# A feed-forward whose first group takes the weights in two halves, and cumulative sums by triangle matmuls

## The chip, the core and the metric

One core of one Trainium2 chip runs one program. Its engines work in parallel, each through its own list of instructions in order: PE (TensorE) multiplies matrices, ACT (ScalarE) evaluates functions, DVE (VectorE) does elementwise work, POOL (GpSimd) only fills constants here, and SP (SyncE) issues all the transfers (DMA). Semaphores tie the lists together. The metric is the time of one execution on the device, in microseconds (us); lower is better.

## The reference

A linear attention with a complex decay is followed by a feed-forward. With 4 batches, 8 heads, 768 time steps and head size 48:

```python
for t in range(S):                      # S = 768
    ar, ai = a_re_n[:, :, t, :, None], a_im_n[:, :, t, :, None]     # capped at magnitude 0.999
    S_re, S_im = ar*S_re - ai*S_im + kv_t, ar*S_im + ai*S_re        # kv_t = outer(k_t, v_t)
    y[:, :, t] = einsum('bhd,bhde->bhe', q[:, :, t], S_re)
x = y.transpose(0, 2, 1, 3).reshape(B * S, H * D)                   # 3072 tokens of 384
h = x @ w_in                                                        # 384 -> 2048, weights in float64
g = maximum(h, 0) + log1p(exp(-abs(h)))                             # softplus
out = g @ w_out                                                     # 2048 -> 384
```

## The kernel before, in words

Time is cut into six *groups* of 128 steps. A group holds 4 *chunks*, one for each batch, of 128 tokens; its 512 tokens go through the feed-forward together. The kernel has two kinds of work.

*Attention.* `pre` turns the decays of a *slice* into running products: the logarithm of the magnitude and the angle of each step (ACT and DVE, 128 features on the partitions), then their cumulative sums over the 128 steps by `TENSOR_TENSOR_SCAN` on DVE (L484), then exp, sine and cosine (ACT), by which q and k are multiplied (L507, L530, L532). The first group has four slices of one batch (tiles 128x384), the others two slices of two batches (128x768). `chunk` then moves q and k to a layout by head with ten small transfers on SP's queue (L567), forms the scores on PE (`sc`, L613), masks them on DVE (L616), forms the outputs (`y`, L644 from the state and L647 from the scores), and casts y to the feed-forward's input `xt` as a rounded part and a rest (L655 or L656, L657). For the next group PE transposes k (`tr`, L590) and adds k's products with v to the state (`kv`, L668).

*Feed-forward.* `moe` takes a group through 16 *steps* of 128 hidden features. A step is nine 128x512 matmuls into a tile `h` (three feature blocks by three products of rounded parts and rests, L703), the softplus (ACT L708 to L710, DVE L711), a split of its result into `gh` and `gl` (L713 on DVE or L714 on ACT, L715 on DVE), and two steps later nine matmuls into the accumulators o0, o1, o2 (L727). There are two tiles `h`, so the third step's first matmul waits until L711 of the first has read its tile. At the end of a group `fin` copies o0 to o2 (DVE L741 and ACT L739) into buffers of the tag "lt", of which there are two, and sends them to the output (L742).

*Weights.* They come as 8-byte numbers in 16 blocks (eight `wi`, eight `wo`, two steps each, 768 KB of raw words). A block takes three DVE instructions on bits (L352, L355, L358), a rounding cast (L365 on ACT, or L367 on DVE) and a subtraction on DVE (L369). `inspect` reads all weights once more (`seen`) for a check on their size; `verdict` adds the checks up at the end with one small matmul (`pn`, L821), and only if one of them had failed a slow general path would run.

*The order.* All this is recorded as tasks with keys from the table `K`. `Planner.order` plays them through with estimated durations, on each engine the ready task of the lowest key first, and the program is written in that order; the engines keep to it whatever the real times are. Where PE has nothing ready between two marks (`gate`, and the first matmul into an accumulator, `opener`) the planner writes in a *filler*, a 128x128 matmul that nobody reads (L753, from L777 of the changed kernel); an f32 matmul of this kind appears as two records in a trace.

Of the kernel before, what the change touches and what calls it, by code (L numbers as in the profile page):

```python
# [21 lines left out]
P = 128  # L22
# [19 lines left out]
NAHEAD = 4  # L42
# [234 lines left out]
class Prog:  # L277
# [15 lines left out]
    def consts(self):  # L293
# [22 lines left out]
        self.toks = dram.tile([B, S, DM], F32, tag="toks", name="toks")  # L316
        self.chk = c.tile([P, self.nchk], F32, tag="chk", name="chk")

    def weights(self):
# [4 lines left out]
        for j in range(2 * NWP):  # L324
# [74 lines left out]
    def pre(self, si):  # L399
# [97 lines left out]
        def acc(j):  # L497
            part = b0 % 2 if m == 1 else None
            a = (car[j], part) if m == 1 else car[j]
            return dict(r=[] if first else [car[j]], w=[] if last else [a])  # L500
# [178 lines left out]
    def moe(self, xt, dst, key, dkey):  # L679
# [404 lines left out]
```

## Time and profile before

| | |
|---|---|
| time, median of 3 runs (lowest to highest) | 626.48 us (623.68 to 626.62) |
| the profiled execution's own time | 620.65 us |
| its span, first to last instruction | 618.9 us |
| PE busy | 577.4 us, 93% |
| DVE busy, ACT busy | 459.7 us (74%), 417.6 us (67%) |
| mean granted PE clock | 0.994 of 2.4 GHz |

The shares are means over stages that differ: PE is filled up from 20 us on, at first largely by fillers, and DVE is nearly full until some 180 us and half empty in the last 100. A row of the stage view gives the busy time of each engine in a stretch of time, so it tells which engine the stretch belongs to.

### The profile page before, as it was taken

To read this page: it belongs to the slowest core of one execution; us is meant where nothing else is said; L and a number is where in the kernel's file an instruction comes from. 1 tells how busy PE (TensorE), PEld (TensorE's weight loads), DVE (VectorE), ACT (ScalarE), POOL (GpSimd) and SP (SyncE) were. 2 spreads that over 40 slices of the span, in tenths; PEclk is the share of its full clock that TensorE was granted. 3 is DMA by queue.
4 is the path that set the end of the run, shared out by engine and by line. 5 is a ranking of instruction groups with operands and counts; after the bars stand their busy time and mean duration, and the time that the engine had idled before them with its cause. 6 is when DMAs were issued, how large, how long until landed. Compare 5 with 4: busy or idle time off the path is not lost.

```text
span 618.9 us, 11061 instructions
## 1 busy us (share of the span) xinstructions
PE 577.4 (93%) x4298; PEld 483.6 (78%) x4298; DVE 459.7 (74%) x702; ACT 417.6 (67%) x769; POOL 1.8 (0%) x16
## 2 busy tenths in 40 slices
PE   0699897999989999999999999999999999999994
PEld 0698886887877888878888888887887788888883
DVE  6898899998987988896778867888784535454442
ACT  8954658668549777785775954869884989345441
POOL 1000000000000000000000000000000000000000
PEclk9999998999999999999999999999999999999998
DMA  8778722252342524341343314251357873010002
GB/s 324 316 166 293 216 88 56 62 169 65 105 138 63 141 85 121 107 103 52 118 117 120 87 30 140 70 181 56 92 154 231 245 235 121 2 51 1 0 2 56
DMA packets 50076, 73.95 MB, mean 119 GB/s; under 512 B 5728, under 2 KB 42080, under 8 KB 50016
## 3 DMA queue, kind: packets, MB, share of 16 engines
q1 hardware_dynamic: 50016, 73.16, 39.0%
q8 instruction: 36, 0.59, 0.4%
q14 instruction: 24, 0.20, 0.1%
HBM read 49.55 MB, written 4.72 MB: 88 GB/s over the span
## 4 chain that ended last, share of the span: by engine, by line
PE 55%; ACT 14%; DVE 12%; DMA 9%; SPq 5%; issue 3%; DVEq 0%; ACTq 0%
PE h L703 21%; PE o L727 20%; SPq L567 4%; DMA x<-dense_dram 4%; PE sc L613 4%; PE o L753 3%; DMA raw_wo<-w_out_dram 3%; ACT L802 3%; PE kv L668 2%; PE y L647 2%; PE y L644 2%; DVE lt L711 2%; ACT lt L710 1%; ACT lt L709 1%; ACT lt L708 1%
## 5 line engine op out<-in xcount | busy, mean ns | idle before, releaser
L703 PE MATMUL h<-xt,wi 128*128 128x512 f32 x864 | 220.6, 401 | 6.7 <-DVE lt L711 6.1
L727 PE MATMUL o<-gh,wo 128*128 128x512 f32 x576 | 197.6, 400 | 0.0
L703 PEld LDWEIGHTS h<-xt,wi 128*128 128x128 f32 x864 | 160.5, 190 | 46.0 <-DVE lt L711 9.1
L711 DVE SCALAR_TENSOR_TENSOR lt<-h,lt 128x512 f32<-128x512 f32 x96 | 66.0, 689 | 96.3 <-ACT lt L710 96.0
L727 PEld LDWEIGHTS o<-gh,wo 128*128 128x128 f32 x576 | 108.5, 188 | 25.5 <-issue 1.2
L708 ACT ACTIVATE lt<-h 128x512 f32<-128x512 f32 x96 | 56.7, 591 | 95.5 <-PE h L703 82.8
L727 PE MATMUL o<-gl,wo 128*128 128x512 f32 x288 | 113.7, 395 | 0.2 <-DVE gl L715 0.2
L710 ACT ACTIVATE lt<-lt,one 128x512 f32<-128x512 f32 x96 | 69.2, 722 | 1.8
L715 DVE TENSOR_TENSOR gl<-lt,gh 128x512 fp32r<-128x512 f32 x96 | 66.2, 689 | 2.0
L727 PEld LDWEIGHTS o<-gl,wo 128*128 128x128 f32 x288 | 54.3, 189 | 11.9 <-DVE gl L715 0.5
L709 ACT ACTIVATE lt<-lt 128x512 f32<-128x512 f32 x96 | 60.6, 633 | 1.8
L613 PE MATMUL sc<-qk 96*128 96x128 f32 x384 | 48.4, 277 | 2.9 <-DMA qk<-x 1.6
L613 PEld LDWEIGHTS sc<-qk 96*128 96x128 f32 x384 | 46.1, 192 | 5.1 <-issue 2.2
L484 DVE TENSOR_TENSOR_SCAN t<-hold,t 128x384 f32<-128x384 bf16 x48 | 43.8, 946 | 2.6 <-ACT t L512 1.9
L713 DVE TENSOR_SCALAR gh<-lt 128x512 fp32r<-128x512 f32 x90 | 38.2, 425 | 9.4 <-PE o L727 3.9
L753 PE MATMUL o<-ident 128*128 128x128 f32 x334 | 41.5, 282 | 0.0
L753 PEld LDWEIGHTS o<-ident 128*128 128x128 f32 x334 | 40.1, 198 | 0.7 <-issue 0.6
L802 ACT ACT_TABLE_LOAD x28 | 35.9, 1283 | 0.4
L616 DVE TENSOR_TENSOR a<-sc,mask 128x512 f32<-128x512 f32 x48 | 31.9, 685 | 4.7 <-PE sc L613 4.5
L668 PEld LDWEIGHTS kv<-v,kt 128*96 128x96 f32 x320 | 29.9, 165 | 3.5 <-ACT s L674 1.4
L668 PE MATMUL kv<-v,kt 128*96 128x64 f32 (+1 forms) x320 | 29.8, 246 | 1.3 <-DMA v<-vpad_dram 1.3
L530 DVE TENSOR_TENSOR x<-x,t 128x1536 f32<-128x1536 f32 (+1 forms) x14 | 21.3, 1526 | 9.5 <-ACT t L517 9.5
(84 smaller groups left out, 585.8 us busy)
## 6 DMA issues: line engine op xcount, KB each, us to landing
x<-dense_dram SPq DMA_DIRECT2D x20, 768.0 KB, 5.4
qk<-x SPq DMA_DIRECT2D x96, 144.0 KB, 3.3
raw_wi<-w_in_dram SPq DMA_DIRECT2D x8, 768.0 KB, 9.6
raw_wo<-w_out_dram SPq DMA_DIRECT2D x8, 768.0 KB, 11.1
seen<-w_in_dram SPq DMA_DIRECT2D x16, 384.0 KB, 3.9
seen<-w_out_dram SPq DMA_DIRECT2D x16, 384.0 KB, 4.3
v<-vpad_dram SPq DMA_DIRECT2D x24, 224.0 KB, 2.8
out_dram<-o SPq DMA_DIRECT2D x18, 256.0 KB, 2.9
```

Of the source, the lines that this page charges most:

```text
L484: V.tensor_tensor_scan(out()[:, s], self.hold, inc()[:, s], 0.0, ALU.mult, ALU.add)
L613: PE.matmul(psc()[:, hh * P : (hh + 1) * P], q[:, h, CH:], q[:, h, :CH], start=True, stop=True)
L668: PE.matmul(kv()[: 2 * D, s], k[:, h, :, :].rearrange("p c d -> p (c d)"), v[:, s], start=h == 0, stop=h == H - 1)
L703: PE.matmul(h()[:, :n], w()[:, q, i, fs], x()[:, i, :n], start=k == 0, stop=k == 3 * NI - 1)
L708: add("ACT", a1(n) - 0.04, lambda: A.activation(tv(), h(), AF.Abs), k, r=[h], w=[t])
L709: add("ACT", a1(n), lambda: A.activation(tv(), tv(), AF.Exp, scale=-1.0), k, w=[t], tab="log")
L710: add("ACT", a1(n, 1), lambda: A.activation(tv(), tv(), AF.Ln, bias=self.one), k, w=[t], tab="log")
L711: add("DVE", d1(n), lambda: V.scalar_tensor_tensor(tv(), h(), 0.0, tv(), ALU.max, ALU.add), k, r=[h], w=[t])
L715: add("DVE", d1(n), lambda: V.tensor_tensor(gl(), tv(), gh().bitcast(F32), ALU.subtract), k, r=[t, gh], w=[gl])
L727: PE.matmul(acc[m]()[:, :n], w()[:, wq, f % 2, ms], x(), start=f == 0 and q == 0, stop=f == NF - 1 and q == 2)
L753: self.nc.tensor.matmul(self.acc0[0]()[:, :P], self.ident, x, start=True, stop=True)
L802: nc.scalar.preload_act_table_set(TABLES[table])
```

## The change

1. The feed-forward runs in seven *segments* instead of six (`SEGS`): the first group with the first eight steps, the second group whole, the first group with its last eight steps, then the other groups. At the end of the first segment its three partial sums go out to a scratch in device memory (`park`); at the end of the third they are read back and added on DVE (L757). 
2. In the first group, the cumulative sums are matmuls with an upper triangle of ones (`sums`, L497 of the changed kernel): the decays of this group now come from the host with time on the partitions, and a product with the triangle sums over time and turns the tile round in one go. The sums stand in PSUM, in tiles borrowed from `h`, o1 and o2, and ACT and DVE read them there. The eight scans of the group go.
3. The gate for fillers is the first triangle matmul instead of a filler behind L507 of the first slice.
4. `fin` takes its copies from the tag "t" (five buffers) instead of "lt" (two), and each copy may go to ACT or DVE.
5. A raw weight block lies in its own block's place instead of another block's or `xt`'s.
6. The table `K` is new throughout, and the planner's constant for a matmul is 0.02 instead of 0.0134 us above its columns.

```diff
-NAHEAD = 4
+SEGS = [(0, 0, NF // 2), (1, 0, NF), (0, NF // 2, NF)] + [(g, 0, NF) for g in range(2, NGRP)]
...
+        self.park = dram.tile([DM, GT], F32, tag="park", name="park")
...
-            shape = [P, n * self.wwords]
-            if j < 2 * NWP - NAHEAD:
-                raw = Buf(self.wpool, f"w{kind}{b + NAHEAD // 2}", shape, I32, f"raw_{tag}")
-            else:
-                raw = Buf(self.p, f"xt{j % 2}", shape, I32, f"raw_{tag}", 2)
+            raw = Buf(self.wpool, tag, [P, n * self.wwords], I32, f"raw_{tag}")
...
-            if not first:
-                V.tensor_tensor(i3[:, :, 0], i3[:, :, 0], car[j](), ALU.add)
+            V.tensor_tensor(i3[:, :, 0], i3[:, :, 0], car[j](), ALU.add)
...
-        st = m * sc(W // m) + (0.1 if first else 0.25)
-
...
-        a = acc(0)
-        add("DVE", st, lambda: scan(0, v1, v1), at(), r=a["r"], w=a["w"] + [t1])
-        add("ACT", a1(W), lambda: A.activation(cc()[:, :, 0, :], n3(v1()), AF.Exp), at(), r=[t1], w=ca, tab="log")
-        add("ACT", a1(W), lambda: A.activation(cc()[:, :, 1, :], n3(v1()), AF.Exp, scale=-1.0),
-            at(), r=[t1], w=ca, tab="log")
...
+        def sums(j, tag, bufs, src, key):
+            ps = Buf(self.ps, tag, [P, 512], F32, f"sum{j}_{si}", bufs)
+            v = lambda: ps()[:, :W]
+
+            def mm():
+                for i in range(NI):
+                    c = slice(i * P, (i + 1) * P)
+                    PE.matmul(ps()[:, c], src[1]()[:, c], self.mask, start=True, stop=True)
+
+            t = add("PE", 0.69, mm, key, r=[src[0]], w=[ps])
+            return ps, v, t
+
+        def keep(j, ps, v, key):
+            c = car[j]
+            add("DVE", 0.1, lambda: V.tensor_copy(
+                c().rearrange("p (i b) -> p i b", b=2)[:, :, b0 % 2], n3(v())[:, :, CH - 1]), key, r=[ps], w=[(c, b0 % 2)])
+
+        if first:
+            lb, vl, opener = sums(0, "h", 2, (t1, v1), at())
+            if si == 0:
+                self.gate = opener
+        else:
+            lb, vl = t1, v1
+            add("DVE", st, lambda: scan(0, v1, v1), at(), r=[car[0]], w=[t1] + ([] if last else [car[0]]))
+        add("ACT", a1(W), lambda: A.activation(cc()[:, :, 0, :], n3(vl()), AF.Exp), at(), r=[lb], w=ca, tab="log")
+        add("ACT", a1(W), lambda: A.activation(cc()[:, :, 1, :], n3(vl()), AF.Exp, scale=-1.0),
+            at(), r=[lb], w=ca, tab="log")
+        if first:
+            keep(0, lb, vl, at())
         add("DVE", d1(2 * W), lambda: V.tensor_tensor(ss(), ss(), cc(), ALU.mult), at(), r=ca, w=sa)
-        if si == 0:
-            self.gate = add("PE", 0.214, lambda: self.filler(sv()[:, :P]), at("turn"), r=sa)
-
...
         def turn():
-            a = acc(1)
-            add("DVE", st, lambda: scan(1, v4, v3), at("turn"), r=a["r"], w=a["w"] + [t3, t4])
-            add("DVE", d2(W), lambda: V.tensor_scalar(vn(), v4(), 1.0 / TWO_PI, None, ALU.mult),
-                at("turn"), r=[t4], w=[t5])
-            add("DVE", d1(W), lambda: V.scalar_tensor_tensor(v3(), v4(), 1.0 / TWO_PI, vn(), ALU.mult, ALU.subtract),
-                at("turn"), r=[t4, t5], w=[t3])
+            if first:
+                ab, va, _ = sums(1, f"o{1 + si % 2}", 1, (t3, v3), at("turn"))
+            else:
+                ab, va = t4, v4
+                add("DVE", st, lambda: scan(1, v4, v3), at("turn"), r=[car[1]], w=[t3, t4] + ([] if last else [car[1]]))
+            add("DVE", d1(W) if first else d2(W), lambda: V.tensor_scalar(vn(), va(), 1.0 / TWO_PI, None, ALU.mult),
+                at("turn"), r=[ab], w=[t5])
+            add("DVE", d1(W), lambda: V.scalar_tensor_tensor(v3(), va(), 1.0 / TWO_PI, vn(), ALU.mult, ALU.subtract),
+                at("turn"), r=[ab, t5], w=[t3])
+            if first:
+                keep(1, ab, va, at("turn"))
...
-    def moe(self, xt, dst, key, dkey):
+    def moe(self, si, f0, f1, xt, dst, parked, key, dkey):
...
-        tmm = n / 2400 + 0.0134
+        tmm = n / 2400 + 0.02
...
                         PE.matmul(acc[m]()[:, :n], w()[:, wq, f % 2, ms], x(),
-                                  start=f == 0 and q == 0, stop=f == NF - 1 and q == 2)
+                                  start=f == f0 and q == 0, stop=f == f1 - 1 and q == 2)
...
             for m in range(NI):
-                ov = o = Buf(p, "lt", [P, GT], F32, "o", NLT)
-                if m == 1:
-                    add("ACT", a1(n), lambda ov=ov, m=m: A.activation(ov(), acc[m](), AF.Copy), k, r=[acc[m]], w=[o])
+                o = Buf(p, "t", [P, NI * 2 * CH], F32, "o", NT)
+                ov = lambda o=o: o()[:, :n]
+                ms = slice(m * P, (m + 1) * P)
+                if f0:
+                    add("SP", 0.45, lambda ov=ov, ms=ms: nc.sync.dma_start(ov(), self.park[ms]),
+                        k - K["plead"], r=[parked[m]], w=[o], nbytes=4 * n * P)
+                    add("DVE", d1(n), lambda ov=ov, m=m: V.tensor_tensor(ov(), acc[m](), ov(), ALU.add),
+                        k, r=[acc[m]], w=[o])
                 else:
-                    add("DVE", d1(n), lambda ov=ov, m=m: V.tensor_copy(ov(), acc[m]()), k, r=[acc[m]], w=[o])
-                add("SP", 0.45, lambda ov=ov, m=m: nc.sync.dma_start(
-                    dst[m * P : (m + 1) * P], ov().rearrange("p (b t) -> p b t", b=B)), k, r=[o], nbytes=4 * n * P)
-
-        for f in range(NF + LAG):
-            if f < NF:
+                    x = add("ACT", a1(n), lambda ov=ov, m=m: A.activation(ov(), acc[m](), AF.Copy), k, r=[acc[m]], w=[o])
+                    x.alt["DVE"] = (d1(n), lambda ov=ov, m=m: V.tensor_copy(ov(), acc[m]()))
+                if f1 < NF:
+                    add("SP", 0.45, lambda ov=ov, ms=ms: nc.sync.dma_start(self.park[ms], ov()),
+                        k, r=[o], w=[parked[m]], nbytes=4 * n * P)
+                else:
+                    add("SP", 0.45, lambda ov=ov, ms=ms: nc.sync.dma_start(
+                        dst[ms], ov().rearrange("p (b t) -> p b t", b=B)), k, r=[o], nbytes=4 * n * P)
+
+        for f in range(f0, f1 + LAG):
+            if f < f1:
                 mm1(f)
-            if f >= LAG:
+            if f >= f0 + LAG:
                 mm2(f - LAG)
         fin()
...
-            for g in range(NGRP):
-                self.moe(self.xt[g], cols[:, :, g * CH : (g + 1) * CH], K["moe"][g], K["step"][g])
+            parked = [Buf(self.p, f"park{m}", [1, 1], F32, f"park{m}") for m in range(NI)]
+            for j, (g, f0, f1) in enumerate(SEGS):
+                self.moe(j, f0, f1, self.xt[g], cols[:, :, g * CH : (g + 1) * CH], parked, K["moe"][j], K["step"][j])
             nc = self.nc
...
 K = {
...
     "moe": [
-        37.01, 124.52, 200.32, 302.35, 357.17, 776.66,
+        39.42, 84.93, 163.49, 185.18, 356.83, 370.86, 421.4,
     ],
     "step": [
-        4.358, 5.33, 6.467, 5.337, 29.837, 52.43,
+        2.126, 3.53, 0.332, 5.405, 0.484, 6.552, 40.863,
     ],
...
-    "backlog": 5173703923634.759,
+    "backlog": 1.925,
...
     for g, b, m in SLICES:
         s = slice(g * CH, (g + 1) * CH)
         for x in (rr, ri):
-            cols.append(x[b : b + m, :, :, s].transpose(2, 1, 0, 3).reshape(P, NI * m * CH))
+            axes = (2, 1, 0, 3) if g else (3, 1, 0, 2)
+            cols.append(x[b : b + m, :, :, s].transpose(axes).reshape(P, NI * m * CH))
         qk = np.stack([x[b : b + m, :, :, s] for x in (rq, rk)], 3)
         cols.append(qk.transpose(2, 1, 0, 3, 4).reshape(P, 2 * NI * m * CH))
     dense = np.ascontiguousarray(np.concatenate(cols, 1))
```

Three places show how the order moves. First PE's list at its start, before the change (o is the accumulator that fillers write, tr the transposes of k, kv the products with v):

```order
L753 MATMUL o_193<-x_96,ident 128x128
L753 MATMUL o_193<-ident 128x128 x33
L590 MATMUL tr_0_261<-ident,x_96 128x128 x3
L753 MATMUL o_193<-ident 128x128 x9
L590 MATMUL tr_1_285<-ident,x_96 128x128 x3
L753 MATMUL o_193<-ident 128x128 x5
L668 MATMUL kv_304<-v_105,kt_270 96x64
```

and after it (sum_0 to sum_3 are the sums of the four slices, first of the logarithms, then of the angles):

```order
L497 MATMUL sum_0_144<-mask,t_104 128x128 x3
L777 MATMUL o_153<-ident 128x128 x2
L497 MATMUL sum_1_164<-mask,t_114 128x128 x3
L777 MATMUL o_153<-ident 128x128 x2
L497 MATMUL sum_0_178<-mask,t_104 128x128 x3
L497 MATMUL sum_1_185<-mask,t_114 128x128 x3
L777 MATMUL o_153<-ident 128x128 x40
L497 MATMUL sum_2_265<-mask,t_122 128x128 x3
L497 MATMUL sum_3_271<-mask,t_148 128x128 x3
L604 MATMUL tr_0_276<-ident,x_97 128x128 x3
```

Ahead of the first feed-forward matmul PE's list has 159 fillers before and 182 now, and 24 triangle matmuls that it did not have; four `kv` now stand there instead of three.

Second, PE's list where the second group's feed-forward begins. Before, in the last rows in front of it (o_841 is an accumulator, y_1679 the output of the second group's last chunk):

```order
L727 MATMUL o_841<-gh,wo_1634 128x512
L727 MATMUL o_841<-gl,wo_1634 128x512
L727 MATMUL o_841<-gh,wo_1634 128x512
L644 MATMUL y_1679<-qk_1478,s_483 32x128 x16
L647 MATMUL y_1679<-a_0_1661,v_1384 32x128 x6
L647 MATMUL y_1679<-a_1_1663,v_1384 32x128 x6
L647 MATMUL y_1679<-a_0_1661,v_1384 32x128 x2
L647 MATMUL y_1679<-a_1_1663,v_1384 32x128 x2
L590 MATMUL tr_0_1720<-ident,x_5_754 128x128 x3
L590 MATMUL tr_1_1725<-ident,x_5_697 128x128 x3
L703 MATMUL h<-xt_1_1481,wi_490 128x512
```

and after the change:

```order
L741 MATMUL o_974<-gh,wo_1341 128x512
L627 MATMUL sc_0_1439<-qk_1322 128x128 x4
L627 MATMUL sc_1_1451<-qk_1322 128x128 x4
L658 MATMUL y_1462<-qk_1322,s_607 32x128 x16
L661 MATMUL y_1462<-a_0_1456,v_1213 32x128 x6
L661 MATMUL y_1462<-a_1_1460,v_1213 32x128 x6
L661 MATMUL y_1462<-a_0_1456,v_1213 32x128 x2
L661 MATMUL y_1462<-a_1_1460,v_1213 32x128 x2
L604 MATMUL tr_0_1495<-ident,x_5_650 128x128 x3
L604 MATMUL tr_1_1500<-ident,x_5_745 128x128 x3
L717 MATMUL h<-xt_1_1113,wi_838 128x512
```

The eighteen accumulator matmuls that stood between the last scores and the last y are no longer there, and this place comes after eight steps of feed-forward instead of sixteen.

Third, DVE's list at the end, before (gl is the last rest, o the copy of an accumulator, good and count belong to the verdict):

```order
L715 TENSOR_TENSOR gl<-lt,gh 128x512
L741 COPY o<-o_5393 128x512
L814 TENSOR_SCALAR good<-chk 128x14 x2
L815 TENSOR_SCALAR good<-chk 128x12
L817 TENSOR_SCALAR good<-chk 128x32
L819 TENSOR_REDUCE n<-good 128x1
L741 COPY o<-o_5401 128x512
L822 CAST count<-pn 1x1
```

and after:

```order
L729 TENSOR_TENSOR gl<-lt,gh 128x512
L761 COPY o<-o_5416 128x512
L839 TENSOR_SCALAR good<-chk 128x14 x2
L840 TENSOR_SCALAR good<-chk 128x12
L842 TENSOR_SCALAR good<-chk 128x32
L844 TENSOR_REDUCE n<-good 128x1
L847 CAST count<-pn 1x1
```

DVE keeps one of the three copies, o1; o0 and o2 are now the last two instructions of ACT before the verdict.

## Rows read from the trace of the kernel before

**Rows 1.** The page, busy time, share and instructions by engine

```profile
PE 577.4 (93%) x4298; PEld 483.6 (78%) x4298; DVE 459.7 (74%) x702; ACT 417.6 (67%) x769; POOL 1.8 (0%) x16
```

**Rows 2.** Stage view: from:to, length, busy (instructions) by engine, clock, DMA, GB/s

```profile
80.00:100.00 20.00, 19.59 (x96) 15.90 (x94) 18.98 (x29) 15.35 (x23) 0.00 (x0) 1.00 0.15 49
100.00:120.00 20.00, 17.12 (x81) 14.12 (x82) 19.59 (x30) 15.34 (x33) 0.00 (x0) 0.91 0.35 91
120.00:140.00 20.00, 20.00 (x180) 17.08 (x179) 19.86 (x30) 11.55 (x24) 0.00 (x0) 1.00 0.39 131
140.00:160.00 20.00, 19.74 (x157) 16.14 (x156) 18.05 (x27) 15.71 (x28) 0.00 (x0) 1.00 0.31 77
...
580.00:600.00 20.00, 20.00 (x88) 16.21 (x87) 9.06 (x15) 8.89 (x14) 0.00 (x0) 1.00 0.00 1
```

**Rows 3.** The chain that ended last: start, length, what; attention and feed-forward on PE

```profile
295.37 1.32 PE kv L668 x16
...
303.01 1.79 PE sc L613 x16
...
306.90 1.01 PE y L644 x32
308.78 2.29 PE h L703 x9
...
559.87 2.08 PE h L703 x9
```

**Rows 4.** PE in order of time, up to the first feed-forward matmul: start, length, instructions

```profile
20.49 0.77 PE L753 MATMUL o<-x,ident 128*128 128x128 f32 x2 [20.49 <-DVE x L507]
...
30.17 2.17 PE L753 MATMUL o<-ident 128*128 128x128 f32 x18
32.18 0.49 PE L590 MATMUL tr<-ident,x 128*128 128x128 f32 x3
...
80.37 4.44 PE L703 MATMUL h<-xt,wi 128*128 128x512 f32 x18
```

**Rows 5.** PE in order of time, its named waits between 100 and 203 us

```profile
102.88 3.75 PE L703 MATMUL h<-xt,wi 128*128 128x512 f32 x9 [3.29 <-DVE lt L711]
...
172.60 1.16 PE L613 MATMUL sc<-qk 96*128 96x128 f32 x8 [1.36 <-DVE s L677]
...
181.47 2.12 PE L703 MATMUL h<-xt,wi 128*128 128x512 f32 x8 [0.53 <-DVE xt L657]
...
202.60 2.35 PE L703 MATMUL h<-xt,wi 128*128 128x512 f32 x9 [0.79 <-DVE lt L711]
```

**Rows 6.** All engines in order of time, the end

```profile
609.40 0.60 ACT L739 ACTIVATE o<-o 128x512 f32<-128x512 f32 x1 [3.56 <-DVE o L741]
609.43 3.89 SPq L742 DMA_DIRECT2D out_dram<-o  x3
...
609.67 0.40 PE L727 MATMUL o<-gh,wo 128*128 128x512 f32 x1
...
612.06 0.69 DVE L741 COPY o<-o 128x512 f32<-128x512 f32 x1 [1.28 <-DMA out_dram<-o]
```

**Rows 7.** The page's groups by line: count, busy us, mean ns, idle before

```profile
L484 DVE TENSOR_TENSOR_SCAN t<-hold,t 128x384 f32<-128x384 bf16 x48 | 43.8, 946 | 2.6 <-ACT t L512 1.9
```

**Rows 8.** DVE in order of time, first group

```profile
11.64 0.55 DVE L474 SCALAR_TENSOR_TENSOR t<-t,x 128x384 f32<-128x384 f32 x1
...
17.16 0.35 DVE L522 TENSOR_SCALAR t<-t 128x384 int32<-128x384 f32 x1
...
42.85 0.55 DVE L655 CAST xt<-y 128x384 fp32r<-128x384 f32 x1
```

**Rows 9.** SP's queue in order of time, transfers of a slice of two chunks

```profile
148.22 11.84 SPq L567 DMA_DIRECT2D qk<-x  x18
```

**Rows 10.** The page's DMA issues: count, KB each, us to landing

```profile
qk<-x SPq DMA_DIRECT2D x96, 144.0 KB, 3.3
...
out_dram<-o SPq DMA_DIRECT2D x18, 256.0 KB, 2.9
```

More of the change, by code (lines that the diff above doesn't have):

```diff
@@ L486, in scan @@
             if not last:
-                if m == 1:
-                    V.tensor_copy(car[j]().rearrange("p (i b) -> p i b", b=2)[:, :, b0 % 2], e)
-                else:
-                    V.tensor_copy(car[j](), e)
+                V.tensor_copy(car[j](), e)
             elif j == 0:
@@ L493, in scan @@
                 V.tensor_copy(chk[:, k : k + n], e)
-        st = m * sc(W // m) + (0.1 if first else 0.25)
[L497 to L500, printed above, removed]
-        a = acc(0)
-        add("DVE", st, lambda: scan(0, v1, v1), at(), r=a["r"], w=a["w"] + [t1])
-        add("ACT", a1(W), lambda: A.activation(cc()[:, :, 0, :], n3(v1()), AF.Exp), at(), r=[t1], w=ca, tab="log")
-        add("ACT", a1(W), lambda: A.activation(cc()[:, :, 1, :], n3(v1()), AF.Exp, scale=-1.0),
-            at(), r=[t1], w=ca, tab="log")
+        st = m * sc(W // m) + 0.25
+        def sums(j, tag, bufs, src, key):
[23 more added lines that the diff above has]
+            keep(0, lb, vl, at())
         add("DVE", d1(2 * W), lambda: V.tensor_tensor(ss(), ss(), cc(), ALU.mult), at(), r=ca, w=sa)
-        if si == 0:
-            self.gate = add("PE", 0.214, lambda: self.filler(sv()[:, :P]), at("turn"), r=sa)
         def arctan():
@@ L704, in mm @@
                         k += 1
-            k = key + f * dkey
+            k = key + (f - f0) * dkey
             add("PE", 9 * tmm, mm, k, r=[xh, xl, w], w=[h])
@@ L727, in mm @@
                         PE.matmul(acc[m]()[:, :n], w()[:, wq, f % 2, ms], x(),
-                                  start=f == 0 and q == 0, stop=f == NF - 1 and q == 2)
-            t = add("PE", 9 * tmm, mm, key + (f + LAG + 0.5) * dkey, r=[gh, gl, w], w=acc)
+                                  start=f == f0 and q == 0, stop=f == f1 - 1 and q == 2)
+            t = add("PE", 9 * tmm, mm, key + (f - f0 + LAG + 0.5) * dkey, r=[gh, gl, w], w=acc)
             if self.opener is None:
@@ L979 @@
     "head": [
-        -560.41, -546.92, 148.37, 531.35, 42.01, 692.43, 447.33, 1993.14, 812.39, 1891.68, 470.77, 1896.28,
-        547.74, 958.53,
+        147.46, 624.17, -734.94, 397.74, -65.21, 161.81, 154.84, 126.74, 332.35, 200.17, 1147.56, 464.07,
+        422.42, 1751.28,
     ],
     "turn": [
-        307.52, 478.0, -1933.13, 1152.69, 1117.53, 1113.2, 1003.08, 756.89, 216.27, 1108.32, 1882.62,
-        1311.56, 639.57, 1147.67,
+        875.87, 931.1, 671.81, 372.5, 881.48, 209.67, 360.72, 269.87, 526.4, 568.29, 228.13, 811.71, 706.01,
@@ L986 @@
+        1996.71,
     ],
     "tail": [
-        -760.62, 28.42, -78.17, 577.44, 60.02, 656.15, 767.27, 1344.42, 751.74, 1456.38, 1532.33, 1463.36,
-        501.03, 514.52,
+        -334.95, 866.41, -128.28, 1028.77, 17.61, 491.11, 317.86, 1067.36, 517.27, 187.54, 259.83, 490.08,
+        795.91, 848.69,
     ],
     "chunk": [
-        -593.21, 1226.55, 701.33, 746.22, 1174.96, 956.09, 1115.27, 1719.46, 294.81, 987.38, 1714.36,
-        1791.33, 956.59, 1028.19, 1243.73, 900.66, 955.7, 1094.05, 809.65, 725.67, 362.78, 1333.35, 545.42,
@@ L994 @@
-        710.1,
+        -267.74, -147.68, 202.11, 211.6, 177.5, 1433.56, 639.03, 1244.43, 174.52, 599.91, 1309.15, 2182.89,
+        343.73, 939.25, 322.68, 1047.42, 1525.38, 564.81, 348.78, 1828.49, 378.39, 329.92, 407.62, 379.87,
     ],
     "state": [
-        -1430.68, -235.25, 60.77, -235.34, 69.33, 71.83, 74.96, 128.39, 133.37, 133.81, 178.76, 167.7,
-        229.8, 214.58, 242.05, 252.5, 310.91, 315.0, 333.03, 333.14, 1051.55, -144.08, 2100.07, -806.27,
+        -1424.69, -194.39, -93.44, -28.82, 43.46, 43.95, 100.96, 52.68, 129.28, 129.32, 145.62, 150.03,
@@ L999 @@
+        185.36, 156.97, 189.71, 254.96, 277.69, 291.22, 297.54, 306.48, 1107.79, 715.4, 146.67, 173.29,
     ],
     "wgt": [
-        -209.85, -176.38, -297.23, 505.85, 451.96, 46.24, -116.72, 60.97, 532.83, 65.07, 64.37, 67.8, 73.01,
-        547.32, 1407.63, 469.93,
+        96.27, -203.72, -101.3, 339.5, -596.58, 402.72, -145.78, 1172.96, 397.64, 873.73, 429.78, 354.94,
+        258.65, 1931.67, 500.63, 58.25,
     ],
     "moe": [
-        37.01, 124.52, 200.32, 302.35, 357.17, 776.66,
+        39.42, 84.93, 163.49, 185.18, 356.83, 370.86, 421.4,
@@ L1006 @@
     ],
     "step": [
-        4.358, 5.33, 6.467, 5.337, 29.837, 52.43,
+        2.126, 3.53, 0.332, 5.405, 0.484, 6.552, 40.863,
     ],
-    "seen": 592.628,
-    "seenstep": 557.383,
-    "rlead": -26.02,
-    "xlead": -247.765,
-    "vlead": -975.165,
-    "backlog": 5173703923634.759,
-    "altpen": 0.873,
-    "tpen": 0.0,
+    "seen": 130.1,
+    "seenstep": 19.706,
+    "rlead": 77.677,
+    "xlead": -372.318,
+    "vlead": -60.991,
+    "plead": -498.518,
+    "backlog": 1.925,
+    "altpen": -0.18,
@@ L1018 @@
+    "tpen": 9.371,
     "table": 1.3,
```

3 lines of the change are left out of this document (1 added, 2 removed).

## The prediction, on record before the changed kernel ran

> **What bounds the kernel now.** I read the busy shares first: PE is at 93% [rows 1], so time can go only where PE stands still, works slowly, or works on nothing. The stage view then shows two kinds of stretch. From 80 to 140 us DVE is busy 58.4 of 60 us, and PE loses 2.9 us of 20 at 100 to 120, where its clock falls too; in the last 100 us DVE is at 45% and PE has no gap [rows 2]. So the front belongs to DVE and the rest to PE. The chain of waits gives PE's prices: 2.09 us for nine feed-forward matmuls, 1.32 for a chunk's kv, 1.79 for its scores, 1.88 for its y (306.90 to 308.78) [rows 3]. There are 192 such nines, 401 us, which the change leaves alone. PE's own list gives the marks: the first filler at 20.49, the first feed-forward matmul at 80.37 [rows 4]. Between them PE mostly runs fillers, that is, it waits. After that its named waits up to 203 us are 3.29 + 1.36 + 0.53 + 0.79 = 6.0 us, and the nine behind the longest take 3.75 instead of 2.35, 1.4 more: 7.4 us lost, nearly all of it to late DVE work [rows 5]. The last view is the end: PE's last matmul ends at 610.07, but the last copy starts at 612.06, held by the transfer that empties its buffer [rows 6].
>
> So the time is the start of the feed-forward, plus PE's work behind it, plus its losses, plus the tail, and I go through these four.
>
> **The start.** The change takes eight scans of 0.95 us off DVE [rows 7] and lets the first weights be five blocks instead of six when the feed-forward begins: counted in the order, that is 8.2 us with their copies and 3.1 for the block, against some 6 us of the second group's instructions that now stand ahead of it: about 5 us less for DVE. That would bring the start to 75, if DVE decided it. But fillers are instructions like others, and PE's list ahead of the first feed-forward matmul got longer: 23 fillers at (32.18 - 30.17) / 9 = 0.22 us [rows 4], 5.1 us; 24 triangles, which are 128x128 f32 matmuls like the fillers, 5.3 us; one more kv, 1.3 us; together +11.7. Against this PE begins earlier: the first triangle needs only the first slice's L474, which ended at 12.2 [rows 8], instead of 20.49: -8.3. Net +3.4 with PE's waits as they are. Some of them should shorten with 5 us less DVE work, and the first triangles may run at the low clock. Bounds: -1 if three or four us of waits go, +7 if sixteen early matmuls at half clock cost 3.5 more. I take +3: the first feed-forward matmul at 83.4.
>
> On those triangles the row says that PE's first two records took 0.77 us together, above the 0.22 of a filler pair [rows 4]. The Trainium skill, TensorE: Matmul & The Clock Gate, section What's actually happening, has the throttled clock as the default which activity releases; by it a sparse early start stays at 1.2 GHz and the term is the upper bound above; with all early matmuls at full clock it would be +3 or less. No row here shows sparse triangles.
>
> The sums are now read from PSUM. The angle's L522 takes 0.35 us for 128x384 from SBUF [rows 8]; four of them from PSUM cost between that and the 0.55 of L655, which reads PSUM at that size: 0 to 0.8 us of DVE, inside the 5 us saved. By the Trainium skill, VectorE: DVE Perf Modes, section Why PSUM operands drop a tier, it would be the upper value, since PSUM has one read port for DVE; by the SBUF row it would be nothing. Neither moves the sum.
>
> **PE's work behind the start.** One kv has moved in front of it (-1.3), and seven filler pairs are left between the first steps where nine stood (-0.4): -1.8 rounded up.
>
> **The losses.** The first segment holds 16 nines (33.4 us), four scores (7.2), four y (7.5), three kv (4.0), and transposes and fillers of some 4: 56 us of PE work. In this stretch DVE's order has 78 instructions; at the mean of rows 2 (76.5 us for 116, 0.66 each) that is 51 us, or 55 with its five widest and six scans counted at their own length. Before, the same 56 us of PE work went with about 96 instructions, 63 us: more than PE had, hence the losses. Now DVE is just below PE. The other half of the weights falls to the first eight steps of the second segment, 33.5 us of PE with no attention among them, and again fills DVE: seven blocks of four instructions and eight softplus tails of three, 52 instructions, 34 us. I expect losses of 4 us where 7.4 were: -3.4. Bounds: -7.4 if DVE never holds PE, +6 if its in-order waits for ACT add up as they do around 102 us.
>
> At the seam between the first two segments the order is tight: behind the last accumulator nine come scores, y, two transposes and the new segment's first h. From the second slice's L544 the chain is 20 transfers at 11.84 / 18 = 0.66 us, 13.2 [rows 9], landing 3.3 [rows 10], half the scores 0.9, mask, y's second half and casts some 3: 20.4 us. PE has five nines, a kv, two scores, two y and transposes for that time, 20.5 us. Even, so 0 to 3 us, inside the 4 above. Behind the waiting h on PE stands everything.
>
> **What costs nothing.** Three more accumulator copies per run and three additions, 0.7 us each: PE has scores, y, three nines and a kv between the last accumulator matmul of the first segment and the next. The six park transfers land in about 2.9 us [rows 10] and have the whole second segment; uncovered it would be under 6. SP gets six issues more among 300. More casts and copies on ACT: it has 200 us free [rows 1]. Raw blocks in their own places: no instruction more, and POOL's list is unchanged.
>
> **The tail.** The third copy no longer waits for a buffer: it can start when PE ends, 610.1 on ACT (0.60) instead of 612.06 on DVE (0.69) [rows 6], and the verdict's matmul behind it comes 2.0 us earlier. Bounds -2.3 and 0. I take -2.0.
>
> **Sum.** +3.0 - 1.8 - 3.4 - 2.0 = -4.2 us, so a span of 614.7 and an own time of 616.4 against 620.65. That execution lies 0.9% under the median of the runs shown, 626.48; by the ratio 0.9932 I predict 622.2 us.
>
> **Rivals.**
> *The longer list eats the gain.* PE paces the front by its fillers, and starts 7 us later; DVE, still at the edge, loses nearly as much as before (-1). +7 - 1.8 - 1 - 2 = +2.2: 628.7 us. For it: PE's list is longer by 11.7 us and in order. Against: before, PE waited in it too.
> *The second group comes late at the seam: slower.* The second group's attention must be done 56 us behind the start; before, it had all 16 steps of the first group. If DVE reaches the second slice's L544 late, each us goes into PE's wait, as PE and chain are even there. Two waits of the kind at 102.88 with their slow nine, 2 x (3.29 + 1.4) = 9.4 us: -4.2 + 9.4 = +5.2, 631.7 us. It decides from about 7 us of DVE idle time in the first segment; before it was 1.6 in 60 [rows 2], with less ACT work beside it.
> *DVE never holds PE again.* Losses go altogether (-7.4) and waits in front shrink (-0.4): -0.4 - 1.8 - 7.4 - 2.0 = -11.6, 614.8 us. For it: 78 instructions instead of 96. Against: DVE and PE are within 5 us of each other over 90 us, and both run in order.
>
> **How the numbers follow.** Forecast 0.40 (617.5 to 626), longer list 0.22, late seam 0.15, no losses 0.23. A measurement of this kernel tells 0.5%, 3.1 us, from no change. Faster by more: 0.30 of the forecast's 0.40 and 0.22 of the no-loss case, 0.52. Slower: 0.14 of the late seam and 0.04 of the longer list, 0.18. The rest, 0.30, is the same. The range 614 to 630 reaches to the rivals on both sides and leaves out the worst of each.
>
> **What would show it.** The first feed-forward matmul at 82 to 85 and the first triangle near 12; fillers in front of it without idle time; waits of h for L725 and of the seam's h for L671 under 4 us together up to 200; the last copy on ACT within 0.2 us of PE's end, and the verdict's matmul at once behind it. I would be wrong if the feed-forward starts before 80 or after 88, or if PE waits over 8 us by the end of the second segment's first half.

## The result, and the profile after

The changed kernel takes 618.43 us, the median of four runs (618.13 to 621.91), against 626.13 (623.68 to 626.62) on the same chip: ratio 0.9897, 95% interval 0.986 to 0.9934. Forecast were 622.2 us and a ratio of 0.9932, so the side is right and the gain 1.5 times as large. In detail the steps came out less well than the sum.

The profiled execution took 621.91 us (span 620.2), the slowest of the four; its span is 1.3 us longer than that of the kernel before (618.9). A second one, e1 below, had a span of 614.0. One execution is not the median, and that becomes part of the answer.

The changed kernel's page, which answers to [rows 1]:

```profile
PE 591.4 (95%) x4388; PEld 497.0 (80%) x4388; DVE 437.6 (71%) x653; ACT 441.8 (71%) x813; POOL 1.8 (0%) x16
```

Its stage view (columns as in [rows 2]):

```profile
80.00:100.00 20.00, 20.00 (x128) 17.51 (x126) 17.91 (x26) 17.25 (x35) 0.00 (x0) 1.00 0.42 112
100.00:120.00 20.00, 20.00 (x217) 16.52 (x216) 19.93 (x27) 16.48 (x25) 0.00 (x0) 1.00 0.29 103
...
220.00:240.00 20.00, 17.22 (x158) 14.31 (x157) 14.70 (x24) 13.84 (x34) 0.00 (x0) 1.00 0.70 210
240.00:260.00 20.00, 20.00 (x144) 16.92 (x143) 14.20 (x19) 14.17 (x23) 0.00 (x0) 0.83 0.12 31
500.00:520.00 20.00, 17.91 (x115) 14.02 (x107) 7.31 (x13) 9.73 (x18) 0.00 (x0) 0.91 0.07 22
```

At 100 to 120 us, where PE lost 2.9 us and clock before, it now has no gap at full clock, though DVE is as full as ever. The trouble has moved to 220 to 260 and 500 to 520, where DVE and ACT have 5 us and more to spare in 20. PE in order of time, its front (start, length, what):

```profile
12.76 1.62 PE L497 MATMUL sum<-mask,t 128*128 128x128 f32 x6 [12.76 <-DVE t L471]
14.17 1.06 PE L777 MATMUL o<-ident 128*128 128x128 f32 x4
...
31.39 0.83 PE L497 MATMUL sum<-mask,t 128*128 128x128 f32 x6
32.06 0.39 PE L777 MATMUL o<-ident 128*128 128x128 f32 x2
...
74.34 7.41 PE L777 MATMUL o<-ident 128*128 128x128 f32 x64
81.51 4.45 PE L717 MATMUL h<-xt,wi 128*128 128x512 f32 x18
```

Each filler or triangle leaves two records. PE works from 12.76 to 81.51 without a named wait, 80.37 before [rows 4]. Next its named waits of 0.4 us or more up to the tail; all of [rows 5] are gone, with one of 0.41 left up to 200 us, and waits at three places behind:

```profile
173.99 0.50 PE L741 MATMUL o<-gl,wo 128*128 128x512 f32 x1 [0.41 <-DVE gl L729]
239.16 1.79 PE L682 MATMUL kv<-v,kt 128*96 128x64 f32 x16 [2.78 <-ACT kt L609]
...
441.82 2.36 PE L717 MATMUL h<-xt,wi 128*128 128x512 f32 x9 [1.51 <-DVE lt L725]
505.03 0.49 PE L717 MATMUL h<-xt,wi 128*128 128x512 f32 x1 [1.31 <-ACT xt L670]
506.31 5.77 PE L717 MATMUL h<-xt,wi 128*128 128x512 f32 x17 [0.78 <-DVE xt L671]
```

(Left out is one of 0.48.) What makes ACT late for the wait at 239 is a check on the size of the weights. SyncE's row, and then ACT's:

```profile
230.45 0.68 SPq L384 DMA_DIRECT2D seen<-w_in_dram  x1
```

```profile
235.76 0.55 ACT L391 ACTIVATE seen<-seen 128x384 f32<-128x384 f32 x1 [4.21 <-DMA seen<-w_in_dram]
236.20 0.48 ACT L670 ACTIVATE xt<-y 128x384 fp32r<-128x384 f32 x1
...
238.66 0.44 ACT L609 ACTIVATE kt<-tr 128x288 f32<-128x288 f32 x1
```

ACT runs in order: it stands 4.21 us for a transfer issued at 230.45, and the cast and the kt that PE needs stand behind it. The wait for the cast xt at 505 follows two checks in the same way: ACT stood 6.10 us for the one at 497.84 and 1.01 for the one at 501.38. That the wait at 441 is the checks' doing is not shown. The tile's rows (count, ns, first and last start) of the kernel before and of the changed one:

```profile
L394 ACT ACTIVATE seen<-seen x32: 528/548/572, 446.0 to 520.5; 128x384 f32<-128x384 f32 x32
```

```profile
L391 ACT ACTIVATE seen<-seen x32: 527/546/577, 147.2 to 577.1; 128x384 f32<-128x384 f32 x32
```

The new table of keys spread the 32 checks from 147 to 577 us; before they stood together, where PE waited at most 0.92 us in that execution (at 482.82). ACT waits 18.0 + 4.2 us for their transfers instead of 3.0 + 2.5. The tail, answering to [rows 6]:

```profile
612.07 0.40 PE L741 MATMUL o<-gh,wo 128*128 128x512 f32 x1
612.51 0.60 ACT L760 ACTIVATE o<-o 128x512 f32<-128x512 f32 x1 [0.80 <-PE o L741]
...
613.33 0.19 PE L846 MATMUL pn<-one,n 128*1 128x1 f32 x2 [0.86 <-DVE n L844]
```

The last copy starts 0.04 us behind PE's last matmul.

**The terms, measured.** Losses here are PE's idle time in the 26 stages of 20 us from 80 to 600, plus (1 - clock) x 20 of each. Work is the time from the first feed-forward matmul to PE's last accumulator matmul, less the losses. All in us against the profiled execution before (span 618.9):

| term | forecast | first execution (620.2) | second, e1 (614.0) |
|---|---|---|---|
| start, 80.37 before | +3.0 | +1.1 | +0.8 |
| work, 518.6 before | -1.8 | -1.4 | -1.8 |
| losses up to 200, 7.6 before | -3.4 | -6.8 | -6.7 |
| losses behind 200, 3.5 before | 0 | +9.4 | +4.0 |
| tail from PE's end, 8.83 before | -2.0 | -1.1 | -1.2 |
| sum | -4.2 | +1.2 | -4.9 |

### The profile page after: what moved, and what is told of

Its sections match the earlier page's. It is cut to its first block, busy times and chain, and to the rows that moved or that the text cites. A ratio compares the mean times of both kernels' runs of the same rounds, so it can differ in the third digit from the quotient of the medians.

```text
span 620.2 us, 11238 instructions
## 1 busy us (share of the span) xinstructions
PE 591.4 (95%) x4388; PEld 497.0 (80%) x4388; DVE 437.6 (71%) x653; ACT 441.8 (71%) x813; POOL 1.8 (0%) x16
## 4 chain that ended last, share of the span: by engine, by line
PE 60%; ACT 14%; DVE 13%; DMA 7%; SPq 3%; issue 2%; DVEq 0%; ACTq 0%
PE o L741 21%; PE h L717 21%; PE sc L627 5%; PE o L777 4%; PE kv L682 3%; DMA x<-dense_dram 3%; ACT L827 2%; SPq L581 2%; DVE lt L725 2%; DMA seen<-w_out_dram 2%; PE y L661 2%; ACT lt L722 1%; PE y L658 1%; DVE t L480 1%; ACT lt L724 1%
## 5 line engine op out<-in xcount | busy, mean ns | idle before, releaser
L717 PE MATMUL h<-xt,wi 128*128 128x512 f32 x864 | 222.9, 403 | 4.7 <-DVE lt L725 2.5
L722 ACT ACTIVATE lt<-h 128x512 f32<-128x512 f32 x96 | 57.0, 594 | 85.9 <-PE h L717 83.6
L627 PE MATMUL sc<-qk 96*128 96x128 f32 x384 | 49.7, 283 | 0.0
L627 PEld LDWEIGHTS sc<-qk 96*128 96x128 f32 x384 | 47.7, 198 | 1.5 <-issue 0.2
L777 PE MATMUL o<-ident 128*128 128x128 f32 x378 | 46.8, 279 | 0.0
L777 PEld LDWEIGHTS o<-ident 128*128 128x128 f32 x378 | 44.7, 195 | 0.6 <-issue 0.6
L480 DVE TENSOR_TENSOR_SCAN t<-hold,t 128x384 f32<-128x384 bf16 x40 | 36.1, 945 | 4.2 <-DMA out_dram<-o 3.3
L391 ACT ACTIVATE seen<-seen 128x384 f32<-128x384 f32 x32 | 17.4, 547 | 22.2 <-DMA seen<-w_out_dram 18.0
```

What stands on the lines that cost most here:

```text
L480: V.tensor_tensor_scan(out()[:, s], self.hold, inc()[:, s], 0.0, ALU.mult, ALU.add)
L627: PE.matmul(psc()[:, hh * P : (hh + 1) * P], q[:, h, CH:], q[:, h, :CH], start=True, stop=True)
L717: PE.matmul(h()[:, :n], w()[:, q, i, fs], x()[:, i, :n], start=k == 0, stop=k == 3 * NI - 1)
L722: add("ACT", a1(n) - 0.04, lambda: A.activation(tv(), h(), AF.Abs), k, r=[h], w=[t])
L777: self.nc.tensor.matmul(self.acc0[0]()[:, :P], self.ident, x, start=True, stop=True)
```

## Experiments

Where fresh runs of the kernel before stand beside an experiment, their median is 625.2 to 625.8 us over 17 to 19 runs (621.8 to 630.8). The edits are shown in extract, with comments added and arguments written out.

**e1, the changed kernel once more.** No edit.

> The changed kernel unaltered, a second execution and more timed runs. Theory: what differs between executions is how long ScalarE stands, in order, for the transfers of the weights' range check (22.2 us in 9 waits in the first profile, the longest 4.2 and 6.1), and TensorE stands behind two of them (2.78 us at 239.16, 2.1 at 505). Then a second profile shows a span of 616 to 618 with these two TensorE waits smaller or elsewhere, and the first feed-forward matmul again at 81.5 within 0.3. Rival: the first profile was slow all over; then the same waits stand at the same places and the missing 3 us are spread over the clock. Both: 618 to 619 us, ratio 0.985 to 0.990.

617.79 us, ratio 0.9873 (0.9838 to 0.9907); the profiled execution has a span of 614.0. PE's list shows the same waits, smaller:

```profile
238.50 1.56 PE L682 MATMUL kv<-v,kt 128*96 128x64 f32 x16 [2.53 <-ACT kt L609]
```

Behind it the clock of 240 to 260 is 0.91 instead of 0.83, the wait at 441 is 0.81 instead of 1.51, of the two at 505 the first is gone, and one for kt (1.14) is new at 382. Losses fell from 13.7 to 8.5 us, which is 5.3 of the 6.2 us between the two. So executions differ in these waits, as the theory has it, though the span is lower than it said and the places mostly stay, which was the rival's. The start was at 81.16.

**e2, the checks later on ACT.** Each check's two activations are put behind up to eight later ACT instructions; no other order changes.

```
+        while k < n and j + 1 < len(out):     # t: a check, n = 8
+            u = out[j + 1]
+            if any(x.tag == b.tag and x.slot == b.slot for x in u.bufs):
+                break
+            j += 1
+            k += u.eng == "ACT"
+        out.insert(j + 1, t)
```

> The changed kernel with each of ScalarE's 32 range checks moved behind up to 8 later ScalarE instructions (fewer where its buffer is wanted earlier); all else in the same order. Theory: the checks' transfers land after ScalarE reaches them, and what stands behind them in ScalarE's order holds TensorE (about 6 us at 239 with the slow stretch behind it, 4 at 505 in the first profile, less in other executions): 3 to 5 us faster than the changed kernel, 613.5 to 615.5 us, no TensorE wait for kt or xt at those places. Rival: ScalarE has 180 us to spare and the waits are hidden, so the time stays at 618.4 within 1.5 us.

615.32 us, ratio 0.9841 (0.9807 to 0.9876), 2.5 us under e1 by the medians, with intervals that overlap. The waits at 239 and 505 are gone, but a new one stands at 175:

```profile
175.13 0.50 PE L766 MATMUL o<-gl,wo 128*128 128x512 f32 x1 [1.94 <-DVE gl L754]
```

The second check had come to stand right ahead of a scan that wanted its buffer, and DVE waited 0.98 us for it. Inconclusive by itself.

**e6, the same without the first two checks.**

```
-    for t in firsts:
+    for t in firsts[2:]:
```

> As e2, but the first two checks, at 147 and 168 us, left where they were: in e2 the second stood right ahead of a scan that wanted its buffer, and TensorE lost 1.94 us and clock for it. Theory: the 2 us of that place come back and the gain of e2 elsewhere stays: 612 to 614.5 us, ratio 0.979 to 0.983, no TensorE wait over 1 us before 600. Rival: e2's gain was none of the checks' doing, or within the scatter; then 616 to 619 us as the changed kernel, ratio 0.986 to 0.990.

611.12 us (610.68 to 614.71), ratio 0.9791 (0.9759 to 0.9822): better than both kernels, below the theory's own range. The stages that were worst:

```profile
220.00:240.00 20.00, 20.00 (x182) 17.32 (x181) 15.74 (x26) 15.59 (x36) 0.00 (x0) 1.00 0.70 209
240.00:260.00 20.00, 18.75 (x148) 14.85 (x147) 15.51 (x21) 16.93 (x31) 0.00 (x0) 1.00 0.22 54
...
500.00:520.00 20.00, 20.00 (x88) 16.22 (x87) 9.05 (x15) 10.90 (x17) 0.00 (x0) 1.00 0.02 6
```

Losses behind 200 us are 3.1 instead of 7.5 in e1 and 12.9 in the first execution, and ACT's waits for the checks' transfers fell from 22.2 us to 1.5. Instructions and data are those of the changed kernel. So the place of 30 checks cost it 6.7 us by the medians of e1 and e6, which come from two chips, and 5.1 by the ratios, whose intervals do not overlap.

**e3, fewer fillers.**

```
+if t.idx == -1:                      # a filler
+    n += 1
+    if n <= 182 and n % 4 == 0:
+        continue
```

> The changed kernel without every fourth of the 182 filler pairs ahead of the first feed-forward matmul: 45 pairs, 45 x 0.22 = 10 us less on TensorE's list. Theory (the prediction's step): TensorE's own list, which runs without a gap from 12.76 to 81.51, sets the start; then the feed-forward starts at 72 to 76 and the time is 609 to 613 us. Rival: the fillers only fill, and VectorE sets the start (its last instruction on the first weights ended at 81.17, and it was busy 37.6 of the 40 us ahead); then the start stays at 80.0 to 81.7, TensorE stands idle some 10 us in front of it, and the time is 618.4 within 2 us, or above by what a lower clock costs.

620.41 us over ten runs (618.4 to 628.59), ratio 0.9956 (0.9915 to 0.9997): not faster than e1, rather slower. PE's list:

```profile
79.09 0.71 PE L717 MATMUL h<-xt,wi 128*128 128x512 f32 x2 [0.60 <-ACT t L524]
80.00 3.29 PE L717 MATMUL h<-xt,wi 128*128 128x512 f32 x13 [0.19 <-DVE wi L366]
...
238.01 2.73 PE L682 MATMUL kv<-v,kt 128*96 128x64 f32 x16 [2.11 <-ACT kt L609]
```

Of 10 us taken off PE's list the start gained 2.1; then it waits for ACT and DVE. The theory's start of 72 to 76 and its time fell; the start lies just under the rival's 80.0, and the time at the edge of the rival's range. By the kv that waits for a check 0.5 us of the 2.1 is left, since a transfer sets that time.

**e10, e6 and e3 together.**

> e6 and e3 together: the checks moved as in e6, and every fourth filler pair ahead of the first feed-forward matmul left out. Theory: thinning the fillers brought the start from 81.2 to 79.1 us in e3, and the 2 us were given back at the kv that waits for a check's transfer at 238 us (238.0 in e3, 238.5 in e1); with that wait gone they stay, 608 to 610 us, ratio 0.974 to 0.978. Rival: fewer fillers cost something of their own behind the start (clock, VectorE), 611 to 615 us, ratio 0.979 to 0.984.

612.99 us, ratio 0.9819 (0.9779 to 0.9859), not faster than e6. The start is at 79.50 against 81.05, but DVE holds PE just behind it: a scores matmul at 199 us stands 0.37 us ahead of that in e6, and the kv at 257.91 only 0.09. Then a wait that was 0.53 in e6 puts PE behind. ACT's row, and PE's:

```profile
420.83 0.85 ACT L482 ACTIVATE t<-x 128x768 f32<-128x768 f32 x1 [2.54 <-DMA x<-dense_dram]
```

```profile
436.81 2.36 PE L742 MATMUL h<-xt,wi 128*128 128x512 f32 x9 [2.40 <-DVE lt L750]
```

The theory falls; fewer fillers gain nothing. The wait at 436 goes back to a late x: ACT stood 2.54 us for it, 0.71 in e6, and what follows on ACT is 1.8 us later up to there. Whether thinning made that transfer late is open.

**e4, an edit that moved more than it meant.** The kernel before, its very last copy into a buffer of tag t.

> The kernel before with one edit: the last of the three accumulator copies of the last group takes its buffer from the five of tag t. Theory (the prediction's step): the last copy starts within 0.2 us of TensorE's end instead of 1.99 behind it, and the end comes 2.0 us earlier, ratio to before 0.9968. Rival: something else holds the end, ratio 1.000. The body in front of 600 us should read as in the kernel before and serves as a second profile of it.

659.12 us, ratio 1.0547. Buffers of a tag are given out in the order of keys, and the checks' keys lie behind that of the copy, so the checks moved to the end: DVE's verdict waits 39.4 us for them. It says nothing on the tail. Its front, in the old order, starts at 79.93 and has waits like [rows 5] (3.15 at 102.11).

**e5, the tail again.**

```
+if last and m == 2:
+    o = Buf(p, "x01", [P, 4 * NI * CH], F32, "o", 2)
```

> The kernel before, the last copy of the last group into a buffer of tag x01, idle by then, instead of one of the two of lt; all else in the same order. Theory (the prediction's step): the last copy starts within 0.2 us of TensorE's end instead of 1.99 behind it, the end comes 2.0 us earlier, ratio to before 0.9968. Rival: another thing holds the end, for one the transfer out, ratio 1.000 and the copy as late as before.

625.19 us against 625.23, ratio 0.9991 (0.996 to 1.0022), which holds both 0.9968 and 1. All engines, the end:

```profile
619.00 0.40 PE L727 MATMUL o<-gh,wo 128*128 128x512 f32 x1
619.43 0.69 DVE L744 COPY o<-o 128x512 f32<-128x512 f32 x1 [0.71 <-PE o L727]
```

The copy does move up by 2 us. But from PE's end to that of the span it is 8.4 us here, 8.8 before, 7.6 to 7.9 in the changed kernel, e1 and e6: a gain of 0.4 to 1.2. What takes the rest, behind the last instruction shown, no row tells.

This profiled execution took 629.57 us, among the slowest of the old order, and shows what such a one loses in front:

```profile
67.74 0.46 PE L613 MATMUL sc<-qk 96*128 96x128 f32 x2 [1.96 <-DMA qk<-x]
...
77.18 0.49 PE L613 MATMUL sc<-qk 96*128 96x128 f32 x2 [1.42 <-DMA qk<-x]
...
82.81 4.44 PE L703 MATMUL h<-xt,wi 128*128 128x512 f32 x18
...
106.29 4.21 PE L703 MATMUL h<-xt,wi 128*128 128x512 f32 x9 [3.27 <-DVE lt L711]
```

The scores wait for qk, up to 12.3 us from issue to landing. Four raw weight blocks had been issued just ahead; DVE first reads them after 87 us.

That is not all it loses. Its span is 8.9 us longer than that of the profiled execution before: 2.4 come from the start, 2.4 from losses up to 200 us, and 4.2 from losses behind 200 (7.7 against 3.5); work and tail change little. The largest of these waits:

```profile
490.61 3.92 PE L703 MATMUL h<-xt,wi 128*128 128x512 f32 x9 [2.07 <-DVE lt L711]
```

DVE waits there for ACT's softplus, which stands behind the checks; for one of them, at 485.40, ACT stood 1.42 us. So the old place of the checks could hold PE too, and the 3.5 of the table is low for the old order: e9 and e11, below, lose 6.1 and 6.3 behind 200.

**e9, the raw blocks behind the qk.** The kernel before, four entries of SyncE's list moved.

```
+held = sp[47:51]; out = [t for t in out if t not in held]
+i = out.index(sp[67]) + 1            # the last qk of the fourth slice
+out = out[:i] + held + out[i:]
```

> The kernel before with four raw weight transfers (issued at 51.3 to 53.4 us, first read by VectorE at 87 us or later) moved on SyncE's queue behind the qk transfers of the third and fourth slice (issued at 54.65 to 73.2). Theory: the executions of the kernel before that take 624 to 629 us, as the one in e5, lose time because qk lands late behind these transfers (up to 12.3 us from issue; TensorE's scores waited 1.96, 1.42 and 0.35 us for it in front and the start came at 82.8 instead of 80.4), and the changed kernel, which issues them after the qk, lost that; then no scores wait for qk before the start, which comes at 78 to 80, and the median falls by 2 to 4 us, ratio to before 0.993 to 0.997. Rival: the slow executions lose it elsewhere (the stretch after 484 us, or all over), ratio 0.999 to 1.001.

626.26 us, ratio 0.9995 (0.9961 to 1.0029). qk now lands within 6.0 us, no scores wait, the start comes at 77.33. But PE, and ACT's row behind it:

```profile
77.33 4.42 PE L711 MATMUL h<-xt,wi 128*128 128x512 f32 x18
...
87.78 4.21 PE L711 MATMUL h<-xt,wi 128*128 128x512 f32 x9 [4.02 <-DVE lt L719]
```

```profile
85.54 0.84 ACT L468 ACTIVATE t<-x 128x768 f32<-128x768 f32 x1 [4.58 <-DMA x<-dense_dram]
```

The moved blocks now delay the next slice's x; ACT stands for it with the softplus queued behind, and all is given back. The edit made a new wait, so the theory stayed open.

**e11, behind the x as well.** sp[70] in place of sp[67].

> As e9, but the four raw transfers stand behind the two x transfers of the next slice too: in e9 the qk came in time and the start fell to 77.3 us, but the x transfer behind the raws landed late, ScalarE stood 4.58 us for it at 85 and VectorE and TensorE behind ScalarE (4.02 us at 87.8). Theory: with x and qk both ahead of the raws that wait goes too and the earlier start stays, ratio to before 0.990 to 0.996, TensorE's waits between the start and 110 us under 3 us. Rival: VectorE sets the pace of the stretch up to 110 us and takes the earlier start back, waits of h for VectorE of 5 us or more there, ratio 0.998 to 1.001.

621.73 us, ratio 0.9941 (0.9916 to 0.9966): 4 us by the order of four transfers alone.

```profile
77.18 4.44 PE L711 MATMUL h<-xt,wi 128*128 128x512 f32 x18
...
100.45 3.91 PE L711 MATMUL h<-xt,wi 128*128 128x512 f32 x9 [3.28 <-DVE lt L719]
```

The time is the theory's. DVE still takes 3.28 us back at 100, so the bound of 3 us that the theory set on the waits failed; but ACT's wait for x is 1.29 and the rest of the earlier start stays.

**e7 and e8, each part alone.** e7 is the changed kernel with `SEGS = [(g, 0, NF) for g in range(NGRP)]`, e8 the changed kernel with the scans of the kernel before for the first group. Both have orders of their own.

> The changed kernel with the first group's feed-forward in one piece again (six segments); triangles, raw blocks in their own places and the copies' buffers as in the changed kernel; the order comes from keys searched anew for it, since neither table fits. Theory (the prediction): the halves take the losses behind the start, the triangles only shorten VectorE's front; without the halves the second half of the weights is again wanted in the first 16 steps, TensorE loses 6 to 8 us behind VectorE between the start and 210 us, and the time is 622 to 625 us, ratio 0.993 to 0.998. Rival: the triangles alone bring VectorE under TensorE, the halves add nothing: losses under 3 us there, 616 to 619 us, ratio 0.986 to 0.990.

> The changed kernel with the first group's sums by VectorE's scans again (data laid out as in the kernel before); two halves, raw blocks and the copies' buffers as in the changed kernel; keys searched anew. Theory (the prediction): eight scans of 0.95 us are back on VectorE ahead of or at the start, 24 triangles (5.3 us) are off TensorE's list; the start moves by under 2 us, VectorE loses its margin and TensorE waits 3 to 6 us more than in the changed kernel up to 210 us: 621 to 624 us, ratio 0.992 to 0.997. Rival: the halves alone bring the gain and the triangles nothing: 616 to 619 us, ratio 0.986 to 0.990.

e7: 621.03 us, ratio 0.9933 (0.991 to 0.9957). e8: 619.32 us, 0.991 (0.9883 to 0.9937). PE's lists, of e7 and then of e8:

```profile
72.06 2.02 PE L627 MATMUL sc<-qk 96*128 96x128 f32 x16 [2.87 <-DMA qk<-x]
...
85.77 4.42 PE L717 MATMUL h<-xt,wi 128*128 128x512 f32 x18
```

```profile
83.89 2.34 PE L700 MATMUL h<-xt,wi 128*128 128x512 f32 x9
...
250.45 1.49 PE L644 MATMUL y<-a,v 128*32 128x128 f32 x20 [2.38 <-DVE a L613]
```

Losses up to 200 us are 0.5 in e7 and 2.0 in e8, 7.6 before. So with either part alone most of them are gone, and the theory's 6 to 8 us for e7 is refuted, though not its ratio. e8's time lies between its two ranges; its start moved by 2.4 us where the theory said under 2, and its losses up to 200 grew by 1.2 where it said 3 to 6. What each pays is a later start, and behind 200 they lose 6.1 and 7.3 (the wait at 250 in e8 is one of these). Start plus losses up to 200, the real worth of a front, is 88.0 before, 86.3 in e7, 85.9 in e8, 82.3 with both and 82.1 in e1. As e7 waits for qk in its own order (2.87 us), the split between the parts is not exact. And one rival is untested: both kernels also have new keys, the raw blocks in their own places and the planner's new constant, and no run has the old structure with keys searched anew. e11 shows that the order of four transfers alone can give a ratio of 0.9941, so how much of the gain belongs to the halves and triangles themselves, and how much to a new order, is not shown.

## Why the prediction was right, and where it was wrong

**The start** (+3.0, measured +1.1 and +0.8). The two ends that made it were there: the first triangle at 12.76 for 12.2, and the early matmuls slow, six records in 1.41 us that take 0.67 later. The waits in front were to shrink in part; they went altogether. That PE's list sets the start is half true: e3 took 10 us off it and won 2.1, then DVE and ACT were the bound. The early pace is as the rule has it that I weighed there (the Trainium skill, TensorE: Matmul & The Clock Gate, What's actually happening). But the +3.5 for it, and with it the +7, had the size wrong, since the kernel before starts slowly too:

```profile
21.05 8.96 PE L753 MATMUL o<-ident 128*128 128x128 f32 x66
29.85 0.49 PE L590 MATMUL tr<-ident,x 128*128 128x128 f32 x3
```

From 20.49 to 29.85 it did 68 records in 9.36 us, which at the later pace (18 in 2.01 us, [rows 4]) take 7.6. The changed kernel did 112 in 15.29 us from 12.76 to 28.05, which at that pace take 12.5. So the slow start costs 2.8 us instead of 1.8, 1.0 more.

**PE's work** (-1.8, measured -1.4 and -1.8) is right.

**The losses** are the step that failed, -3.4 as a net sum. I put DVE just below PE and left 4 us of losses up to 200; 0.8 and 0.9 were left. Up to there my rival, DVE never holds PE again, is what happened. The seam that I had as even shows no wait at all. With the start, the front won 5.7 us where the sum had 0.4. Behind 200 us I had nothing, and there 4.0 to 9.4 us more were lost than in the one execution before: the new keys moved the checks, a part of the change that I did not price, and e6 shows it by taking that cost away, down to 3.1 us of losses. Against e5's 7.7, e1's 7.5 would be no increase. Two errors of opposite sign hid each other, so that -4.2 lies near e1's -4.9 is luck.

**What costs nothing.** The park transfers landed in 2.1 and 3.1 us by the median and 5.3 at most, and no instruction waited for one. The angle's reads from PSUM cost the upper value:

```profile
L534 DVE TENSOR_SCALAR t<-sum x4: 544/548/557, 18.7 to 41.9; 128x384 int32<-128x384 f32 x4
```

0.55 us against 0.35 from SBUF [rows 8]: 0.8 us in four, as the Trainium skill, VectorE: DVE Perf Modes, section Why PSUM operands drop a tier, would have it.

**The tail** (-2.0). The mechanism is right to 0.04 us, the worth was 1.1 and 1.2.

**From the execution to the median.** I scaled by the ratio. But the profiled execution before, 620.65 us, lies below the 17 to 19 runs taken beside each experiment, while e1's, 615.7, is the fastest of six and the difference of medians is 7.4 us there. The sum from the profile, -4.9 in e1, holds no more than what that execution had to lose. e5 shows what another execution lost: 4.8 us more in front, with late qk, and 4.2 behind 200. In neither profiled execution of the changed kernel does a scores matmul wait for qk ahead of the start: five of its raw blocks are issued at 67 to 76 us, behind the fourth slice's qk. e11 prices such a step at 4 us in the old order. That qk makes up the 2.5 us between -4.9 and -7.4 is argued, not shown: no trace of the kernel before lies at its median, and the losses behind 200 are a rival.

**What I said would show me wrong**, a start before 80 or after 88, or 8 us of waits by the end of the second segment's first half, did not come; the start missed its 82 to 85 by 0.5.

## What to carry to other kernels

An engine that runs in order stands for the latest transfer in its list, and everything behind it stands too: work that nobody waits for belongs behind what PE needs, and after its data has surely landed (the checks' transfers took 3.0 to 7.0 us here). When a table of keys changes, compare where every kind of instruction now stands, not only those that the change names. And see where the profiled execution lies among the timed runs before summing against it.

## Not expected of the hardware

The first triangles run at half pace, six records in 1.41 us at 12.76 and in 0.67 at 31.39, near the ratio of 1.2 and 2.4 GHz, with PE idle up to 12.76; yet the column of the granted clock says 1.00 there. Behind the wait at 239 the same column falls to 0.83 over 20 us. So the early pace is read from the rows. And the same order on the same data has fronts that differ between executions: up to the feed-forward e4 and e5 have the order of the kernel before, and it starts at 79.93 and 82.81, with 80.37 in the profiled execution before. The waits of scores for qk are longest in e5. Between 40 and 85 us qk took up to 11.9 us to land in the execution before and 12.3 in e5, and 5.9 in the changed kernel, with most of the raw blocks behind it.
